# Chunked attention and a token mixer on one core: q, k and v loaded as flat rows, value products in four quadrants, and a new order of work

## The chip, the cores and the metric

The kernel runs on one core of one Trainium2 chip. The metric is the device time of one execution in microseconds (us), as the median of several runs. A profile is one execution taken by the hardware profiler; its span runs from the first to the last instruction. The engines are called PE (matrix products; PEld is its weight load), DVE (vector), ACT (scalar), POOL (GpSimd) and SP (sync). Arithmetic on PE is in f16 with sums in f32 in PSUM, which has eight banks.

## The reference, cut to what matters

Attention inside chunks of 64 tokens, for 8 batches, 8 heads, 576 tokens (nine chunks) and a head size of 64, then a mixer over all tokens of a batch:

```python
scores = scale * np.matmul(q_c, k_c.transpose(0, 1, 2, 4, 3))   # (B, H, 9, 64, 64)
scores = scores - np.max(scores, axis=-1, keepdims=True)
attn = np.exp(scores)
attn = attn / (np.sum(attn, axis=-1, keepdims=True) + 1e-09)
out = np.matmul(attn, v_c)
x = out.transpose(0, 2, 1, 3).reshape(B, S, H * D)              # (8, 576, 512)
wq = x @ w_q                                                    # (8, 576, 64)
wk = x @ w_k
W_tok = scale * np.einsum('bsd,btd->bst', wq, wk)
mixed = np.einsum('bst,btd->bsd', W_tok, x)
return (np.maximum(mixed, 0.0) @ w_out).astype(np.float32)
```

Inputs and output are f32. q, k and v are 9.4 MB each, the output is 9.4 MB, `w_out` is 1 MB.

## The kernel before, in words

**Order.** `ORDER` is a list of words written out by hand, such as `SC2.0@0` or `OE5:A`: a kind of step, a batch (or an output tile), a part, the first PSUM bank after `@`, the engine after `:`. The loop at the end of the kernel goes through it and issues each step's instructions; every engine runs its own in that order. The mixer is computed as `wq @ (wk^T x)`, so nothing of size 576 x 576 is made.

**Loads** (`load`, L100 to L124). q, k and v are brought in by POOL, which casts f32 to f16 on the way. The heads of a batch are split in two halves: heads 0 to 3 go to partitions 0 to 63 (f = 0), heads 4 to 7 to partitions 64 to 127 (f = 1). Each transfer fills one half, 64 partitions. q and k go in blocks of 512 rows, eight consecutive rows to a partition (L113), and the last 256 rows of a half as a tail of four rows to a partition (L120). v goes one row of 64 numbers to a partition (L108). A batch takes ten transfers or more. All q and k have a buffer (four pairs of batches, `qk`); v has five buffers, `vt`, and batch n + 5 is loaded when the value products of batch n have been issued. The output tiles are staged in the `qk` buffers of batches that are done, and the first store waits for the last load (`last["held"]`).

**v buffers** (`clear`, L126). A `vt` buffer holds, for each pair of chunks g, 132 columns: the values of half 0 on partitions 0 to 63 in columns 0 to 63, those of half 1 on partitions 64 to 127 in columns 66 to 129, a column of ones behind each (it gives the sum of the exponentials), and zeros elsewhere. DVE clears two of the five buffers and POOL three, between the loads.

**A batch** runs through these steps.

- TR (`tr`, L156; its instruction is at L174): DVE transposes 32 x 32 blocks of q and k from `qk` to `qkT`, as f32 words that hold two f16. For q the columns are also reordered so that the writes are runs of eight words; for k and the tails the writes go in steps of eight or four words. Three parts with 512, 512 and 128 columns, for q and k each.
- SC (`sc`, L179, product at L188): scores of 64 keys by 64 queries. The head size lies in 32 words of two numbers (e = 0, 1), so a score is the sum of two products with 32 rows. Four strips of 32 rows (i = 0 to 3) are used in turn.
- EX (`ex`, L196): ACT takes the exponential out of PSUM into `est`; for 1024 columns with a reorder that undoes q's.
- PV (`pv`, L205, product at L217): one product for a pair of chunks, one of each half: 128 rows (64 keys of each), 64 queries, 130 columns of `vt`. Forty in a batch.
- RN (`rn`, L227): DVE takes the reciprocals of the sums (L231) and multiplies (L232), giving `xn`, the attention output in f16.
- DT (`dt`, L241): DVE transposes `xn` in 32 x 32 blocks to `xq`.
- PJ (`pj`, L245), EP, DU, WT, EW: the projections with `w_q` and `w_k` (64 products on four strips), their copy out of PSUM, a copy of half of it to the other partitions, and the transposition of `wk` on PE with its copy by DVE.
- GM (`gm`, L284), EG: `wk^T x` and its copy out.
- MX, RL: `wq` times that, and the relu into `rmx`, four parts (ACT, at the end DVE too).
- OM, OE (`oe`, L347): the product with `w_out`, 128 tokens at a time (36 tiles, four products of 512 columns each), the copy out of PSUM, and, when a group of tiles is full, its store by SP (L357).

Scores and value products of a batch, its mixer and output tiles of earlier batches are interleaved, so that PE has work while DVE and ACT work on other parts.

## Time and profile before

| what | value |
|---|---|
| runs | 142.51, 146.77 and 146.08 us; median 146.08 |
| span of the profiled execution | 144.6 us; the times around the span are not listed for it, so this stands for its time, 1.5 us under the median |
| PE | 2312 products with as many weight loads |
| DVE, ACT | 172 and 105 instructions |
| last load lands, first store is issued | at 97 us, at 98.4 us |
| last product ends, last copy out of PSUM starts | 138.5 us |

How to read the rows. A row of the groups gives line, engine, operation, what it writes and reads with partitions x elements, the count, then busy time in us and the mean ns of one, then the idle time of the engine before them and what ended it. A row of the timeline gives start, duration, engine, line, operation, count, and in brackets the idle time before it. A row of the chain of waits gives start, duration, engine, line, count; "issue" is time in which the engine waited for nothing that the profile shows. A row of the windows gives the stretch, its length, busy time and instruction count of each engine, the granted clock of PE, the DMA share and GB/s. GB/s count the bytes written, f16 for the loads.

### The profile page before, as it was taken

To read this page: it belongs to the slowest core of one execution; us is meant where nothing else is said; L and a number is where in the kernel's file an instruction comes from. 1 tells how busy PE (TensorE), PEld (TensorE's weight loads), DVE (VectorE), ACT (ScalarE), POOL (GpSimd) and SP (SyncE) were. 2 spreads that over 40 slices of the span, in tenths; PEclk is the share of its full clock that TensorE was granted. 3 is DMA by queue.
4 is the path that set the end of the run, shared out by engine and by line. 5 is a ranking of instruction groups with operands and counts; after the bars stand their busy time and mean duration, and the time that the engine had idled before them with its cause. 6 is when DMAs were issued, how large, how long until landed. Compare 5 with 4: busy or idle time off the path is not lost.

```text
span 144.6 us, 5246 instructions
## 1 busy us (share of the span) xinstructions
PE 99.5 (69%) x2312; PEld 58.9 (41%) x2312; DVE 90.5 (63%) x172; ACT 65.5 (45%) x105; POOL 68.8 (48%) x105
## 2 busy tenths in 40 slices
PE   0022763147697849987699874998984999989920
PEld 0021642036455523655445552355453356643400
DVE  5643791384896649888917989378971597455100
ACT  4410301032746624584343625467752376564630
POOL 7957996994699781793783883600000000000000
PEclk9999999999999995998557999689999599999997
DMA  4999899999699999999999999995996050441295
GB/s 98 151 186 191 54 172 187 144 184 203 79 148 146 201 154 184 173 144 182 177 151 195 180 147 197 174 102 233 410 408 268 17 208 5 175 190 74 75 360 218
DMA packets 51782, 25.11 MB, mean 174 GB/s; under 512 B 38608, under 2 KB 49872, under 8 KB 51760
## 3 DMA queue, kind: packets, MB, share of 16 engines
q0 software_dynamic: 49056, 14.69, 103.2%
q1 hardware_dynamic: 2704, 10.09, 17.6%
q8 instruction: 18, 0.29, 0.8%
q14 instruction: 4, 0.03, 0.1%
HBM read 29.62 MB, written 9.44 MB: 270 GB/s over the span
## 4 chain that ended last, share of the span: by engine, by line
PE 54%; DMA 12%; issue 10%; POOL 9%; ACT 7%; DVE 3%; DVEq 0%; ACTq 0%; POOLq 0%
PE pb L339 26%; PE pb L217 9%; DMA vt<-in_v_dram 8%; PE pb L188 7%; PE pb L250 5%; DMA qk<-in_q_dram 5%; POOL qk L113 4%; PE pb L288 4%; ACT est L203 3%; POOL vt L108 3%; PE pb L303 2%; ACT rmx L317 2%; POOL vt L129 1%; POOL qk L120 1%; DVE xn L232 1%
## 5 line engine op out<-in xcount | busy, mean ns | idle before, releaser
L339 PE MATMUL pb<-wout,rmx 128*128 128x512 f16 x144 | 40.2, 420 | 0.9 <-ACT rmx L317 0.9
L174 DVE STREAM_TRANSPOSE qkT<-qk 128x512 f32<-128x512 f32 (+1 forms) x48 | 31.2, 717 | 13.7 <-DMA qk<-in_q_dram 11.1
L188 PE MATMUL pb<-qkT 32*64 32x64 f16 x1152 | 16.7, 210 | 24.6 <-DVE qkT L174 18.1
L203 ACT ACTIVATE est<-pb 128x1024 f16<-128x1024 f32 (+1 forms) x24 | 19.2, 813 | 30.6 <-PE pb L188 30.1
L232 DVE TENSOR_TENSOR xn<-pb,rec 128x768 f16<-128x768 f32 (+1 forms) x32 | 26.4, 824 | 4.3 <-PE pb L288 3.2
L351 ACT COPY qk<-pb 128x512 f32<-128x512 f32 x34 | 19.8, 587 | 20.1 <-PE pb L339 19.4
L188 PEld LDWEIGHTS <-qkT 32*64 32x64 f16 x1152 | 13.8, 123 | 28.5 <-DVE qkT L174 19.9
L217 PE MATMUL pb<-vt,est 128*64 128x130 f16 x320 | 18.7, 258 | 9.6 <-ACT g L297 2.8
L108 POOL DMA_DIRECT2D vt<-in_v_dram x20 | 20.9, 1055 | 7.8 <-DMA qk<-in_q_dram 3.2
L339 PEld LDWEIGHTS <-rmx 128*128 128x128 f16 x144 | 13.5, 108 | 16.3 <-issue 4.0
L217 PEld LDWEIGHTS <-est 128*64 128x64 f16 x320 | 12.9, 127 | 16.5 <-issue 7.9
L317 ACT ACTIVATE rmx<-pb 128x576 f16<-128x576 f32 x28 | 17.0, 653 | 4.6 <-PE pb L303 4.5
L231 DVE RECIPROCAL rec<-pb 128x12 f32<-128x12 f32 (+1 forms) x32 | 6.6, 206 | 16.3 <-PE pb L217 16.1
L243 DVE STREAM_TRANSPOSE xq<-xn 128x384 f32<-128x384 f32 (+1 forms) x32 | 15.2, 497 | 0.7
L120 POOL DMA_DIRECT2D qk<-in_k_dram x16 | 8.3, 530 | 11.8 <-DMA vt<-in_v_dram 10.4
L250 PE MATMUL pb<-xq,wpj 32*128 32x160 f16 x512 | 12.3, 242 | 1.9 <-DVE xq L243 1.2
L113 POOL DMA_DIRECT2D qk<-in_q_dram x18 | 11.2, 627 | 2.6 <-DMA qk<-in_k_dram 1.3
L250 PEld LDWEIGHTS <-wpj 32*128 32x128 f16 x512 | 10.1, 97 | 5.3 <-issue 5.0
L261 ACT CAST wqk<-pb 128x640 f16<-128x640 f32 x8 | 5.5, 693 | 14.0 <-PE pb L250 14.0
L113 POOL DMA_DIRECT2D qk<-in_k_dram x18 | 11.1, 633 | 0.0
L120 POOL DMA_DIRECT2D qk<-in_q_dram x16 | 8.8, 575 | 1.1 <-DMA vt<-in_v_dram 1.1
L303 PE MATMUL pb<-wqk,g 64*128 64x288 f16 x32 | 8.4, 309 | 1.2 <-ACT rmx L317 0.7
(24 smaller groups left out, 57.5 us busy)
## 6 DMA issues: line engine op xcount, KB each, us to landing
out_dram<-qk SPq DMA_DIRECT2D x11, 768.0 KB, 4.3
qk<-in_q_dram POOLq DMA_DIRECT2D x14, 256.0 KB, 7.1
qk<-in_k_dram POOLq DMA_DIRECT2D x14, 256.0 KB, 8.5
vt<-in_v_dram POOLq DMA_DIRECT2D x12, 288.0 KB, 7.1
vt<-in_v_dram POOLq DMA_DIRECT2D x8, 144.0 KB, 5.3
out_dram<-qk SPq DMA_DIRECT2D x3, 256.0 KB, 2.0
qk<-in_q_dram POOLq DMA_DIRECT2D x4, 128.0 KB, 5.1
qk<-in_k_dram POOLq DMA_DIRECT2D x4, 128.0 KB, 5.7
```

Of the source, the lines that this page charges most:

```text
L108: d = nc.gpsimd.dma_start(vt[b % NVB][rows, NCH * lo : NCH * hi, f * (D + 2) : f * (D + 2) + D], src.rearrange("(c p) d -> p c d", p=CH)[: ...
L113: d = nc.gpsimd.dma_start(qk[b // 2][rows, b % 2, s, 8 * lo : 8 * hi].rearrange("p (t r) d -> p t (r d)", r=8), src[0 : 4 * 512].rearrange ...
L120: d = nc.gpsimd.dma_start(qk[b // 2][rows, b % 2, s, 32:36].rearrange("p r d -> p (r d)"), src[4 * 512 :].rearrange("(p r) d -> p (r d)", ...
L174: nc.vector.transpose(out=to, in_=frm)
L188: nc.tensor.matmul(ps[half : half + CH, bank + i % 2, at : at + CH], lhsT=qkT[b % 2][rows, 1, tok, e], rhs=qkT[b % 2][rows, 0, tok, e], st ...
L203: nc.scalar.activation(dst, src, AF.Exp, scale=scale_attn)
L217: nc.tensor.matmul(ps[CH * o : CH * o + CH, bank + m // 3, at : at + VP].rearrange("p (f d) -> p f d", f=2)[:, :, 0 : D + 1], lhsT=e, rhs= ...
L232: nc.vector.tensor_tensor(out=xn[b % 2][:, 6 * u : 6 * u + nb * ns // 2].rearrange("p (k n) (f d) -> p k (n f) d", k=nb, f=2), in0=xv[:, : ...
L250: nc.tensor.matmul(ps[:, bank + i, 0 : NJ * 32], lhsT=wpj[32 * i : 32 * i + 32, 4 * f + kk, e, :], rhs=xq[b % 2][32 * i : 32 * i + 32, NJ ...
L317: nc.scalar.activation(dst, src, AF.Relu, scale=scale_moe)
L339: nc.tensor.matmul(ps[:, bank, :], lhsT=c[:, r], rhs=wout[:, i, :], start=(i == 0), stop=(i == NI - 1),)
L351: nc.scalar.copy(os_, ps[:, bank, :])
```

## The change

Ahead of attention, rows are addressed flat over heads, (h s), without the split in halves. A load spans 128 partitions: q and k take four consecutive rows to a partition, for all 4608 rows in nine blocks of 512, without a tail; v takes one row to a partition. Batch 0 comes in six transfers, the others in three, and `w_out` in one. There are eight v buffers of 66 columns per chunk (64 values, a one, a gap), without zeros, so that all loads are issued at the start without waiting for a buffer, and the clears go; only the ones are set, by DVE.

A chunk of 64 rows now lies on half of the partitions: chunk n = 9 h + c is at partitions 64 (n mod 2) on. So a value product takes 64 rows, and its result goes to partitions 64 (c mod 2) on: four quadrants of PE's array, 72 products of 65 columns in a batch. Scores go to four units of 32 or 40 products, each of which uses two strips of rows and both halves of the columns. q and k are transposed by steps of their own (TQ, TK) in parts of 512 and 640 columns, all in the form of the old tails. There are four exponentials of 512 and 640 columns without reorder, four normalisations of equal size, two back transposes of 640 columns. The order is new as a whole; some EW, EG, RL and OE change engine. New words `ZZ` are filler products of 512 columns on a tile of ones whose result nobody reads: 79, of which 67 stand ahead of the first projection.

```diff
 ORDER = """
-TR0.0 SC0.0@0 EX0.0 PV0.0@2 TR0.1 TR0.2 SC0.1@4 RN0.0 SC0.2@6 EX0.1 DT0.0 PV0.1@0 EX0.2 PV0.3@2 RN0.1 PV0.2@4
-RN0.3 DT0.1 DT0.3 RN0.2 DT0.2 PJ0@0 TR1.2 TR1.0 SC1.2@6 EP0 EX1.2 SC1.0@4 TR1.1 WT0@0 EX1.0 PV1.3@1 EW0 RN1.3
...
+ZZ1@0 ZZ1@1 ZZ1@2 ZZ1@3 ZZ1@4 ZZ1@5 ZZ1@6 ZZ1@7 TQ0.0 TK0.0 ZZ13@0 SC0.0@0 SC0.1@2 EX0.0 EX0.1 ZZ4@4 PV0.0@2 RN0.0
+TQ0.1 TK0.1 ZZ14@4 SC0.2@2 SC0.3@0 EX0.2 EX0.3 ZZ1@4 PV0.1@2 RN0.1 ZZ1@4 PV0.2@0 PV0.3@4 DT0.0 RN0.3 TQ1.0 TQ1.1
+RN0.2 DT0.1 TK1.0 ZZ26@6 PJ0@0 TK1.1 SC1.0@4 EP0 SC1.1@6 EX1.1 WT0@0 DU0 SC1.3@2 EW0:D EX1.0 SC1.2@6 GM0@0 EX1.2
...
-    vt = [sb.tile([P, NG, VP], F16, name=f"vt{i}") for i in range(NVB)]
+    vt = [sb.tile([P, NG, VP], F16, name=f"vt{i}") for i in range(B)]
...
-    halves = [x.rearrange("b (f h) s d -> b f (h s) d", f=2) for x in (q, k, v)]
+    flat = [x.rearrange("b h s d -> b (h s) d") for x in (q, k, v)]
...
+            src = flat[s][b]
+            if s == 2:
+                d = nc.gpsimd.dma_start(
+                    vt[b][:, lo:hi, 0:D],
+                    src.rearrange("(g p) d -> p g d", p=P)[:, lo:hi, :],
+                )
+            else:
+                d = nc.gpsimd.dma_start(
+                    qk[b // 2][:, b % 2, s, 4 * lo : 4 * hi].rearrange(
+                        "p (t r) d -> p t (r d)", r=4
+                    ),
+                    src.rearrange("(t p r) d -> p t (r d)", p=P, r=4)[:, lo:hi],
+                )
...
+    def tr(b, x, s):
+        at = (slice(0, 16), slice(16, NG), slice(0, 8), slice(8, 16))[x]
+        nc.vector.transpose(
+            out=qkT[b % NQT][:, s]
+            .bitcast(F32)
+            .rearrange("p n o -> p (n o)")[:, 32 * at.start : 32 * at.stop]
+            .rearrange("p (t w r) -> p t r w", r=4, w=32),
+            in_=qk[b // 2][:, b % 2, s, at].bitcast(F32).rearrange("p (t r) w -> p t r w", r=4),
+        )
...
     def sc(b, u, bank):
+        pi = u % 2
+        for x, t in enumerate(((0, 1, 2, 3), (4, 5, 6, 7, 8))[u // 2]):
+            for e in range(2):
+                for row in (2 * pi, 2 * pi + 1):
+                    for eta in range(2):
+                        rows = slice(32 * row, 32 * row + 32)
+                        half = slice(CH * eta, CH * eta + CH)
+                        tok = slice(P * t + CH * eta, P * t + CH * eta + CH)
                         nc.tensor.matmul(
+                            ps[half, bank + row % 2, CH * x : CH * x + CH],
+                            lhsT=qkT[b % NQT][rows, 1, tok, e],
+                            rhs=qkT[b % NQT][rows, 0, tok, e],
...
     def pv(b, u, bank):
+        for c in range(NCH):
+            for h in (2 * u, 2 * u + 1):
+                n = NCH * h + c
+                eta, o = n % 2, c % 2
+                t, row = n // 8, (n % 8) // 2
+                e = est[b % 2][2 * (t >= 4) + row // 2][
+                    CH * eta : CH * eta + CH, row % 2, t % 4 if t < 8 else 4
+                ]
+                at = VP * (c // 2)
                 nc.tensor.matmul(
+                    ps[CH * o : CH * o + CH, bank + h % 2, at : at + D + 1],
                     lhsT=e,
+                    rhs=vt[b][CH * eta : CH * eta + CH, n // 2, 0 : D + 1],
...
+    def idle(n, bank):
+        for _ in range(n):
+            nc.tensor.matmul(
+                ps[:, bank, :], lhsT=unit[:, 0:P], rhs=unit[:], start=True, stop=True
+            )
+
+    nc.vector.memset(unit[:], 1.0)
+    for i in range(B):
+        nc.vector.memset(vt[i][:, :, D : D + 1], 1.0)
+    load(0, ["q0-4", "k0-4", "v0-18", "q4-9", "k4-9", "v18-36"])
     small_weights()
-    clear(2, "G")
-    load(1, ['q0-4', 'k0-4', 'q4-5', 'k4-5', 'v0-4'])
+    load(1, ["q0-9", "k0-9", "v0-36"])
+    make_identity(nc, ident[:])
     weights()
...
+    for b in range(2, B):
+        load(b, ["q0-9", "k0-9", "v0-36"])
```

More of the change, by code (lines that the diff above doesn't have):

```diff
@@ L40 @@
+OE33:A OE35:A
 """.split()
@@ L62 @@
     NJ = (NCH + 1) // 2
[L63 to L65 removed]
+    NG = H * NCH // 2
     NI = DM // P
     HS = S // 2
[L68 removed]
+    VP = D + 2
     scale_attn = 1.0 / math.sqrt(D)
@@ L141 @@
+            last["i"] = d
+    def weights():
+        nc.gpsimd.dma_start(wout[:], moe_w_out.rearrange("(i p) m -> p i m", p=P))
     wpf = rmx[1][:].rearrange("p i n -> p (i n)").bitcast(F32)[0:32, 0 : 16 * 2 * DH].rearrange(
@@ L391 @@
             banks[kind, n, x] = int(bank)
-        if kind == "TR":
-            tr(n, x)
+        if kind == "TQ":
+            tr(n, x, 0)
+        elif kind == "TK":
+            tr(n, x, 1)
         elif kind == "SC":
@@ L399 @@
             pv(n, x, banks["PV", n, x])
-            left[n] = left.get(n, 4) - 1
-            if left[n] == 0 and n + NVB < B:
-                load(n + NVB, VL[n + NVB])
-                if n + NVB + 1 < B:
-                    load(n + NVB + 1, QKL)
         elif kind == "RN":
@@ L430 @@
             oe(n, banks["OM", n, 0], eng)
+        elif kind == "ZZ":
+            idle(n, int(bank))
     tc.add_manual_dep(
```

247 lines of the change are left out of this document (77 added, 170 removed).

## The prediction, on record before the changed kernel was seen

> **What bounds the kernel now.** I read the page's engine shares and chain first, then one window per stage, then the single waits.
>
> ```profile
> span 144.6 us, 5246 instructions
> PE 99.5 (69%) x2312; PEld 58.9 (41%) x2312; DVE 90.5 (63%) x172; ACT 65.5 (45%) x105; POOL 68.8 (48%) x105
> q8 instruction: 18, 0.29, 0.8%
> PE 54%; DMA 12%; issue 10%; POOL 9%; ACT 7%; DVE 3%; DVEq 0%; ACTq 0%; POOLq 0%
> ```
>
> ```profile
> 28.00:62.00 34.00, 25.56 (x660) 15.81 (x661) 25.31 (x49) 16.48 (x28) 24.58 (x39) 0.95 1.58 162
> 62.00:97.00 35.00, 28.19 (x697) 16.31 (x699) 26.89 (x52) 17.48 (x29) 21.18 (x32) 0.80 1.74 168
> 97.00:139.00 42.00, 37.76 (x721) 20.46 (x720) 23.78 (x46) 25.17 (x43) 0.00 (x0) 0.96 0.48 190
> ```
>
> The columns of the windows are PE, PEld, DVE, ACT and POOL busy, granted clock, DMA share and GB/s. No engine is full over the whole run. Up to 62 us the transposes wait for q and k, which the next rows show; after that the loads are ahead, and PE, 81% to 90% busy, sets the pace.
>
> ```profile
> 7.02 0.71 DVE L174 STREAM_TRANSPOSE qkT<-qk 128x512 f32<-128x512 f32 x1
> 7.89 1.09 DVE L174 STREAM_TRANSPOSE qkT<-qk 128x512 f32<-128x512 f32 x1 [0.16 <-DMA qk<-in_k_dram]
> 28.08 1.90 DVE L174 STREAM_TRANSPOSE qkT<-qk 128x128 f32<-128x128 f32 x3 [0.30 <-DMA qk<-in_k_dram]
> 62.07 1.12 DVE L174 STREAM_TRANSPOSE qkT<-qk 128x512 f32<-128x512 f32 x1 [0.85 <-DMA qk<-in_k_dram]
> ```
>
> The four rows are q and k of batch 0, k of batch 1 and k of batch 4: DVE stood still until they landed. The last one is the last time that a load holds the kernel up.
>
> The "issue" tenth of the chain is a second bound. Two rows of PE's timeline (first and last of the six relu-layer products) and the chain around them:
>
> ```profile
> 48.40 0.29 PE L303 MATMUL pb<-wqk,g 64*128 64x288 f16 x1
> ...
> 48.79 0.28 PE L303 MATMUL pb<-wq,g 64*128 64x288 f16 x1
> ```
>
> ```profile
> 43.08 0.98 PE pb L339 x4
> ...
> 45.12 1.05 issue
> 46.17 0.28 PE pb L188 x10
> 46.45 0.47 PE pb L217 x12
> 46.92 0.66 PE pb L288 x10
> 47.59 0.24 PE pb L217 x4
> 47.83 0.68 PE pb L188 x64
> ...
> 49.60 0.99 PE pb L217 x21
> 50.60 2.14 issue
> 52.74 0.28 PE pb L217 x3
> ```
>
> Both waits split a group of products in the middle (6 and 10 of 16, 21 and 3 of 24), with nothing that releases them. Between them lie 10 + 12 + 10 + 4 + 64 + 6 + 21 = 127 products, that is 254 instructions with a weight load each. The page's instruction queue made 18 transfers of 0.29 MB together, and PE runs 2312 + 2312 = 4624 instructions, 257 to a transfer. So I read these waits as PE standing at the end of a block of 256 instructions whose successor has not arrived. The longest of each kind:
>
> ```profile
> PE pb L188 <- issue: 6.4, 4, 2.5
> PE pb L217 <- ACT g L297: 2.8, 2, 1.4
> PE pb L217 <- issue: 2.1, 1, 2.1
> ```
>
> The middle row is put down to ACT, but both waits lie a multiple of 256 instructions from the others. Seven waits, 11.3 us: 0.63 us for each of 18.1 blocks, about 1.6 us where a block ends in a run of short products.
>
> ```profile
> 68.00:77.50 9.50, 8.37 (x190) 0.50 1.69 171
> ...
> sum 18.30, PE 17.17; mean PE 4.29
> ```
>
> Last, in four stretches, 18.3 us in all, the granted clock was 0.50; PE was busy for 17.17 us of them.
>
> **The change part by part.** The sum is made against the span of 144.6 us, which is 1.5 us under the median of the three runs (146.08); I add the 1.5 back at the end.
>
> *Loads.* Ninety transfers become 28, and q and k rows go in runs of four (512 B in f16) where they went in runs of eight (1024 B) with tails. Three stretches of the DMA queues and two idle ones (the windows' last column):
>
> ```profile
> DMA packets 632, 0.61 MB, mean 205 GB/s; under 512 B 32, under 2 KB 632, under 8 KB 632
> ```
>
> ```profile
> DMA packets 298, 0.20 MB, mean 200 GB/s; under 512 B 45, under 2 KB 297, under 8 KB 297
> ```
>
> ```profile
> DMA packets 2268, 0.29 MB, mean 144 GB/s; under 512 B 2268, under 2 KB 2268, under 8 KB 2268
> ```
>
> ```profile
> 16.50:18.50 2.00, 1.55 (x28) 1.30 (x24) 1.05 (x3) 0.96 (x2) 2.00 (x5) 1.00 0.38 26
> ...
> 37.50:39.50 2.00, 1.10 (x20) 0.64 (x14) 1.93 (x4) 1.92 (x4) 1.98 (x2) 1.00 0.20 26
> ```
>
> ```profile
> L129 POOL MEMSET vt<- 128x2376 f32 x3 | 6.3, 2096 | 0.0
> ```
>
> Over 16 engines a 1024 B packet costs 16 x 1024 / 205 = 80 ns and a 128 B packet of v 16 x 128 / 144 = 14 ns. A straight line gives 42.5 ns for 512 B, 193 GB/s. It is 205 at best; solving the mixed row in the middle for its short packets, with its waste, gives about 161 at worst. A batch is 1.18 MB of q and k and 0.59 MB of v: 6.1 + 4.1 = 10.2 us, all of it back to back, since POOL's clears (2.1 us each, during which nothing is issued and the queues run dry to 26 GB/s) and the waits for v buffers are gone. POOL's own work per batch falls under 10 us, so it hides under the transfers. Batch 4's k needs 5 x 6.1 + 4 x 4.1 + 2.6 for wout = 49.5 us plus start and landing; batch 0's first 0.52 MB (2.6 us) had landed at 7.9, so at most 5.3, and I take 4.5 because no clear and fewer issues stand ahead. It lands at 54 where it landed at 62.1: **-8.1 us** (-9 at 205 GB/s; -2 at 161). Batch 1's k lands at 2 x 6.1 + 4.1 + 4.5 = 20.8 instead of 28.1.
>
> *What is late next.* DVE works 90.5 / 8 = 11.3 us a batch, about 11.0 without its clears, longer than the loads' 10.2. Over batches 2 to 4 it falls behind by 3 x 0.8: **+2.4 us** (0 if its idle time covers it; 5 if PE's waits add to it).
>
> *Transposes and their layout.* The rows of DVE and ACT that price them:
>
> ```profile
> L174 DVE STREAM_TRANSPOSE qkT<-qk 128x128 f32<-128x128 f32 x16 | 5.4, 393 | 8.4 <-DMA qk<-in_q_dram 7.2 <-DMA qk<-in_k_dram 1.2
> L243 DVE STREAM_TRANSPOSE xq<-xn 128x384 f32<-128x384 f32 x24 | 13.0, 563 | 0.5
> L243 DVE STREAM_TRANSPOSE xq<-xn 128x128 f32<-128x128 f32 x8 | 2.4, 302 | 0.2
> L203 ACT ACTIVATE est<-pb 128x1024 f16<-128x1024 f32 x16 | 16.3, 1026 | 20.7 <-PE pb L188 20.1 <-ACT qk L351 0.4
> L203 ACT ACTIVATE est<-pb 128x256 f16<-128x256 f32 x8 | 3.1, 388 | 10.0 <-PE pb L188 10.0
> ```
>
> q lost nothing in the old layout (0.71 us for 512, against k's 1.09), but both now take the form of the tails, whose 128 columns cost 393 ns where a plain transpose costs 302. On k's line, (1090 - 393) / 384 = 1.8 ns an element, 640 columns take 1.32 us: a batch is 2 x (1.09 + 1.32) = 4.82 instead of 2 x (0.71 + 1.09 + 0.39) = 4.38, +0.44. The back transposes, two of 640 (302 + 512 x 1.02 = 824 ns) for three of 384 and one of 128, give back 0.34. Four batches lie behind the last load wait: **+0.4 us** (0 to +1.8). Four exponentials of 512 and 640 columns cost 2 x 0.60 + 2 x 0.71 = 2.62 for 2.44, and the normalisation the same columns; ACT is 53% busy from 28 us on and hides it (0.7 us if not). The engines of EW, EG, RL and OE change hands one for one: zero, covered by DVE's and ACT's idle time, 3 us if that is gone.
>
> *Value products.* Forty of 128 rows and 130 columns become 72 of 64 rows and 65 columns in four quadrants. Now twelve take 0.47 us, 39 ns each, 1.57 a batch. The nearest row for the new ones is that of the scores, 64 columns each, 64 products in 0.68 us, 10.6 ns; the upper end is the old 39 ns. I take 13 ns, since a quadrant must load and stream by itself (52 ns over four): 0.94 a batch, **-2.5 us** over the four batches behind the load waits (-3.2; +5 at 39 ns). That two column halves of the same rows run together is shown: a product of 512 columns takes 0.98 / 4 = 245 ns, so 130 columns alone would need 62 ns, and they took 39.
>
> The Trainium skill, "TensorE: Matmul & The Clock Gate", Part 3, says that a weight load overlaps products in flight only when its row group differs, which speaks against this order of quadrants and of scores; the 39 ns do not bear that out for column halves, and the rule's own result is a rival below.
>
> *Instructions.* PE's go from 4624 to 2 x 2647 = 5294 (256 more value products, 79 filler products): 2.6 blocks more, at 0.63 us each **+1.6 us** (0 if the extra blocks end in long products, +6 at the 2.1 us above).
>
> The Trainium skill, "Runtime: NRT & Kernel Launch", Instruction fetch mechanics, calls the crossing of such a block mostly hidden; by that the term would be 0 and the time 138.3. The 2.14 us wait says otherwise here.
>
> *Fillers.* 67 of 79 filler products stand ahead of the first projection. At 245 ns the 26 before it take 6.4 us; they hide under the wait for batch 1's k (20.8) and cost up to 4 us if the clock is at half there. DVE's transposes of q1 now stand ahead of the last normalisation of batch 0, so projection 0 waits for that landing too; the scores of batch 1 had to wait for it anyway. The eight ones columns and the filler operand delay DVE by no more than the two old clears. SP's stores wait for the last load and so start near 89 instead of 98, at no cost on the path. The new order as such I put at 0 (-4 to +4).
>
> Sum: -8.1 + 2.4 + 0.4 - 2.5 + 1.6 = -6.2; 144.6 becomes 138.4, and with the 1.5, **139.9 us**.
>
> **The rivals.**
>
> *Blocks set the pace (slower).* Counting the new order in blocks of 256 from the same start, eleven boundaries after batch 0 fall behind runs of scores and value products; now seven waited. If each waits 2.3 us (2.14 and 2.5 are above), that is 25.3 us instead of 11.3 + 1.6: 152 us. It turns slower than 149 from a mean of 2.0 us. For it: the value products finish faster, so less time for the fetch. Against: loads end sooner, and today's mean is 1.6.
>
> *Row groups serialise.* A score strip does 16 products in 0.64 us, 40 ns each; the new units use two strips at a time, so scores would cost 2.9 a batch instead of 1.5, and value products 36 x 40 = 1.44 instead of 0.94: +7.6 over four batches, less 1.6 since the fetch then has time: 146. Against it stand the 39 ns. This is the page's rule named above.
>
> *Loads come no earlier.* At 161 GB/s a batch takes 11.4 us, batch 4's k lands at 60, and DVE keeps pace: 139.9 + 6.1 - 2.4 = 143.6. For it: packets half as long.
>
> *The waits shrink.* Fillers hold the clock (half of the 8.6 us that 17.17 at half clock cost, 4) and the waits at blocks fall from 11.3 to about 6 as packets ahead of the fetch get shorter: 131. Against: the fetch waited 2.5 us in the stores' time too.
>
> **How the numbers follow.** Forecast 0.36 (134 to 144), blocks 0.17, row groups 0.12, loads 0.13, shrinking waits 0.22. The range of 130 to 150 leaves out the upper half of the block rival and the tail below. Two per cent, about what a measurement of this kernel can tell from no change, is 143.2 to 149.0. Faster: nearly all of the forecast, the shrinking waits and half of the loads rival, 0.62; same: row groups, the other half, the edges, 0.21; slower: 0.17.
>
> **What would show it.** Right: batch 1's k at about 21 us, batch 4's near 54, the last load near 89; q and k at 185 to 200 GB/s; 18 value products in about 0.24 us; a 512-column transpose at 1.09 us; "issue" waits near 13 us. Wrong: a k4 landing after 58; score units of 32 products at over 0.5 us; "issue" over 20 us; projection 0 later than 26 us.

## The result, and the profile after

The changed kernel took 151.55 us (median of 4 runs, 150.47 to 152.51), beside 146.43 us (142.51 to 147.84) for the kernel before on the same chip: a ratio of 1.059 with a 95% interval of 1.041 to 1.077. Executions of one kernel fall into a faster and a slower group some per cent apart, so the ratios here and below are taken over the faster ones alone and the medians over all, and the trace of the kernel before, with its span of 144.6 us, is by that length one of the slower. It is slower by some 6%, where 139.9 us had been forecast, and it lies above the forecast's range of 130 to 150. The profiled execution took 152.51 us, 150.7 of them in the span.

Page of the changed kernel: span, engines, granted clock in 40 slices, the instruction queue, the chain by engine.

```profile
span 150.7 us, 5753 instructions
...
PE 119.1 (79%) x2647; PEld 65.5 (43%) x2647; DVE 93.0 (62%) x146; ACT 65.6 (44%) x110; POOL 33.7 (22%) x34
...
PEclk9999879965599857996555697589955999999999
...
q8 instruction: 20, 0.33, 0.8%
...
PE 59%; issue 13%; DVE 9%; ACT 8%; DMA 7%; POOL 2%; DVEq 0%; ACTq 0%; POOLq 0%
```

The same clock line of the kernel before:

```profile
PEclk9999999999999995998557999689999599999997
```

"issue", time in which the engine waited for nothing that the profile shows, is 13% of the chain (10% before). The clock is at half in more slices, 51.2 us against 20.5, but these two figures can't be set side by side. The trace of the kernel before has no clock record ahead of 36.9 us, and the page counts that stretch as full speed. The products there came at the rate of half clock; these are 64 score products ahead of 36.9 us and 64 behind it:

```profile
33.64 1.07 PE L188 MATMUL pb<-qkT 32*64 32x64 f16 x64
...
43.99 0.71 PE L188 MATMUL pb<-qkT 32*64 32x64 f16 x64
```

Score products came every 13.2 ns from the first one at 9.04 us on, and every 8.2 ns later. From 36.9 us on the comparison is fair: 42.0 us at half clock against 20.5. The longest "issue" pieces and their neighbours in the chain:

```profile
19.70 6.33 PE pb L333 x26
26.03 1.28 PE pb L214 x64
...
29.03 3.70 issue
...
48.31 3.57 issue
...
63.24 1.01 PE pb L214 x45
64.26 4.23 issue
68.49 0.71 PE pb L214 x18
...
79.51 1.65 issue
```

26 filler products, then projection 0 at 26.03 us (19.3 us before). The wait of 4.23 us cuts projection 3 in two, 45 products and 18. Counted in the trace's records of PE (each product, its weight load, and a few semaphore records), these waits end at instructions 961, 1729, 2241 and 2753 of 5294, all 193 more than a multiple of 256, as do three shorter ones: 15.7 us in seven waits, 11.3 us in seven before. I call what lies between two such places a block.

DVE's waits for loads, after and before:

```profile
DVE qkT L139 <- DMA qk<-in_q_dram: 4.9, 2, 3.3
```

```profile
DVE qkT L174 <- DMA qk<-in_q_dram: 11.1, 3, 5.2
DVE qkT L174 <- DMA qk<-in_k_dram: 2.5, 5, 0.9
```

So the loads did come earlier: by the trace's completion signals, k of batch 1 landed at 23.1 us (28.0 before) and k of batch 4 at 56.0 (62.0 before); the last packet of a load ended at 88.6 (98.0 before). 8.7 of the 13.6 us in the last two rows are gone. Both waits of the first row are for batch 0's q; from batch 1 on no transpose waits for a load.

The work behind did not follow. The first transpose of batch 4's k, which waited for its load until 62.07 us before, is this piece of the chain in the changed kernel, 16.8 us after its k had landed:

```profile
72.78 1.08 DVE qkT L139
```

The new order has put somewhat more work ahead of it. But at 62.07 us itself PE was no further either: it had begun 512 score products, three projections and 34 output products in the kernel before, and 500, two and 36 in the changed one.

Where did the time go? Two windows each, cut about where the loads end (columns as above: busy time of PE, PEld, DVE, ACT, POOL, granted clock, DMA share, GB/s). After:

```profile
26.00:88.00 62.00, 46.35 (x1228) 26.72 (x1227) 39.26 (x56) 27.09 (x47) 16.95 (x13) 0.72 1.79 180
88.00:146.00 58.00, 50.54 (x1149) 29.10 (x1137) 39.68 (x65) 32.29 (x56) 0.00 (x0) 0.88 0.37 146
```

Before:

```profile
19.00:97.00 78.00, 56.57 (x1419) 34.05 (x1422) 55.67 (x110) 34.66 (x57) 53.35 (x78) 0.89 1.68 167
97.00:138.00 41.00, 37.31 (x720) 20.46 (x720) 23.78 (x46) 24.45 (x42) 0.00 (x0) 0.96 0.48 188
```

The 0.89 in the first row of the kernel before counts 19 to 36.9 us as full clock, which it was not. When its loads end, the kernel before has 720 products left, the changed one 1149. Counted at the block that begins there:

| | before | after |
| --- | --- | --- |
| block begins, us | 97.23 | 87.85 |
| instructions behind it | 1359 of 4624 | 2285 of 5294 |
| projections, score and output products left | 3, 232, 84 | 4, 432, 96 |
| from there to the last product, us | 41.2 | 58.4 |
| PE busy / idle in it, us | 37.5 / 3.7 | 51.0 / 7.5 |
| of it at half clock, us | 3.4 | 13.7 |

The block begins 9.4 us earlier, and what is left takes 17.2 us longer: the last product ends 7.8 us later (146.3 instead of 138.5), of which a shorter tail (4.4 us for 6.2) gives 1.7 back: the 6.1 us between the spans. The end of the loads came nearer; the work did not come with it.

Are these waits the fetching of instructions? The trace has the packets of the instruction queue, one of 16384 bytes for each block. Each of the seven waits of either kernel ended 1.3 to 1.6 us after such a packet had ended, and the packet itself took 0.9 to 1.4 us, with loads or without. So they are waits for the next block of instructions. What differs is when its packet starts:

| kernel, block begins at, us | next block's packet starts after, us | it takes, us | from its end to the next block, us |
| --- | --- | --- | --- |
| after, 45.41 | 4.09 | 0.97 | 1.41 |
| after, 62.02 | 4.10 | 1.07 | 1.30 |
| after, 74.69 | 4.03 | 0.97 | 1.48 |
| after, 87.82 (first behind the loads) | 0.92 | 0.93 | 1.41 |
| after, 105.24 | 1.29 | 0.96 | 1.32 |
| before, 103.22 (stores running) | 4.81 | 0.94 | 1.44 |

### The profile page after: what moved, and what is told of

Its sections match the earlier page's. It is cut to its first block, busy times and chain, and to the rows that moved or that the text cites. A ratio compares the mean times of both kernels' runs of the same rounds, so it can differ in the third digit from the quotient of the medians.

```text
span 150.7 us, 5753 instructions
## 1 busy us (share of the span) xinstructions
PE 119.1 (79%) x2647; PEld 65.5 (43%) x2647; DVE 93.0 (62%) x146; ACT 65.6 (44%) x110; POOL 33.7 (22%) x34
## 4 chain that ended last, share of the span: by engine, by line
PE 59%; issue 13%; DVE 9%; ACT 8%; DMA 7%; POOL 2%; DVEq 0%; ACTq 0%; POOLq 0%
PE pb L306 27%; PE pb L214 8%; DMA qk<-in_q_dram 7%; PE pb L333 6%; PE pb L156 6%; PE pb L183 4%; PE pb L252 3%; ACT rmx L286 3%; DVE xn L195 3%; DVE qkT L139 3%; PE pb L270 3%; ACT est L166 2%; ACT wqk L223 1%; POOL qk L111 1%; DVE rec L194 1%
## 5 line engine op out<-in xcount | busy, mean ns | idle before, releaser
L166 ACT ACTIVATE est<-pb 128x512 f16<-128x512 f32 (+1 forms) x32 | 19.5, 652 | 23.7 <-PE pb L156 19.2
L195 DVE TENSOR_TENSOR xn<-pb,rec 128x640 f16<-128x640 f32 x32 | 26.4, 824 | 1.2
L333 PE MATMUL pb<-unit 128*128 128x512 f16 x79 | 24.9, 462 | 1.5 <-DVE unit L337 1.5
L194 DVE RECIPROCAL rec<-pb 128x10 f32<-128x10 f32 x32 | 6.6, 206 | 27.5 <-PE pb L183 25.4
L183 PE MATMUL pb<-vt,est 64*64 64x65 f16 x576 | 13.0, 220 | 7.2 <-issue 4.7
L183 PEld LDWEIGHTS <-est 64*64 64x64 f16 x576 | 10.2, 127 | 11.5 <-issue 7.0
L204 DVE STREAM_TRANSPOSE xq<-xn 128x640 f32<-128x640 f32 x16 | 13.4, 836 | 0.4
L333 PEld LDWEIGHTS <-unit 128*128 128x128 f16 x79 | 8.2, 111 | 12.3 <-issue 5.4
L270 PE MATMUL pb<-wq,g 64*128 64x288 f16 x32 | 9.8, 363 | 0.0
L111 POOL DMA_DIRECT2D qk<-in_k_dram x9 | 8.8, 973 | 1.5 <-DMA qk<-in_q_dram 1.5
## 6 DMA issues: line engine op xcount, KB each, us to landing
wout<-in_moe_w_out_dram POOLq DMA_DIRECT2D x1, 512.0 KB, 18.1
```

Of the source, the lines that this page charges most:

```text
L166: nc.scalar.activation(est[b % 2][u].rearrange("p i n c -> p i (n c)"), ps[:, bank : bank + 2, 0:n], AF.Exp, scale=scale_attn,)
L183: nc.tensor.matmul(ps[CH * o : CH * o + CH, bank + h % 2, at : at + D + 1], lhsT=e, rhs=vt[b][CH * eta : CH * eta + CH, n // 2, 0 : D + 1] ...
L195: nc.vector.tensor_tensor(out=xn[b % 2][:, 2 * u : 2 * u + 2], in0=xv[:, :, :, 0:D], in1=rc[:, :, :, None].broadcast_to([P, 2, NJ, D]), op ...
L270: nc.tensor.matmul(ps[:, bank + h, 0:HS], lhsT=g16[b % 2][CH * h : CH * h + CH, i * P : i * P + P], rhs=src[CH * h : CH * h + CH, half * H ...
L333: nc.tensor.matmul(ps[:, bank, :], lhsT=unit[:, 0:P], rhs=unit[:], start=True, stop=True)
```

## The experiments

I began with two theories: A, that PE stands at the ends of blocks because the next block's transfer is held up behind the loads; B, that the new order's dependences cost it by themselves. C (the clock follows the use of the array), F (under the loads the blocks set a pace, whatever is in them) and others came later. Ratios are against the kernel before on the same chip; the changed kernel itself was not run again beside its variants, so they are set beside it by their ratios. Where only a few lines of a repeated edit are shown, the rest is as the expectation says.

**Loads taken away.** Both kernels without the loads of batches 2 to 7, computing on the data of batches 0 and 1. The clears of the v buffers that are no longer used go too, and the stores start at 40 to 42 us instead of 89 to 98.

```diff
-        src = qk[b // 2][:, b % 2].bitcast(F32)
+        src = qk[0][:, b % 2].bitcast(F32)
...
-    for b in range(3, NVB):
-        load(b, QKL + VL[b])
-    load(NVB, QKL)
```

> The kernel before, without the loads of batches 2 to 7 (their steps compute on the q, k and v of batches 0 and 1, so the output is not the reference's). Theory A (PE stands at the end of blocks of 256 instructions because the next block's transfer is held up behind the loads, and the clock halves after such waits): the seven long waits of 11.3 us fall under 3 us, the time at half clock from 20 us to under 10, and the kernel takes about 128 us. Theory B (the waits are dependences between the engines, and loads matter only where a transpose waits for them): the gain is the 13.6 us that DVE waited for q and k, less what compute makes up, about 140 us, and the long waits of PE stay near 11 us.

> The changed kernel, without the loads of batches 2 to 7 in the same way. Theory A: the seven waits of 15.7 us fall under 3 us, the time at half clock from 51 us to under 20, and the kernel takes about 126 us, level with the quiet kernel before or under it. Theory B (the new order and layout are worse by themselves): it stays about 5 us above the quiet kernel before, at 140 us or more, with the clock at half for some 50 us.

Measured: 127.57 us for the one (145.08 for the kernel before, ratio 0.886, interval 0.875 to 0.898), 142.45 and 145.07 us for the other. In the kernel before the seven waits are gone, and the clock is at half for 3.4 us from its first clock record at 35.6 us on: A holds there. In the changed kernel the first block behind instruction 3009 begins at 74.97 us instead of 87.85, but 7.8 us of waits at blocks' ends stay, and 33 us at half clock from 35.6 us on. The first transpose of batch 4's k is at 62.72 us, later than in the kernel before with all its loads.

```profile
PE pb L157 <- issue: 3.0, 2, 1.9
PE pb L184 <- issue: 1.9, 2, 1.1
...
PE pb L215 <- issue: 1.6, 1, 1.6
```

So A alone does not tell the two kernels apart: the changed kernel has a floor of its own some 15 us above the old one's, and above the forecast of 139.9 us. What the order, the layout and the clock each have in that floor was not measured. It has blocks of little but scores and value products that end in a wait, loads or not, though without loads they begin only 2.8 to 5.3 us apart.

**The order mended by hand, and without fillers.** Eleven output tiles moved between score units (first block); all but the first eight filler products taken out (second).

```diff
-SC2.0@0 TK2.1 EX2.0 WT1@4 DU1 SC2.3@6
+SC2.0@0 OM0@6 TK2.1 EX2.0 WT1@4 DU1 OE0:A OM1@5 SC2.3@6
```

```diff
-TQ0.0 TK0.0 ZZ13@0 SC0.0@0
+TQ0.0 TK0.0 SC0.0@0
```

> The changed kernel with the same instructions; ten output tiles are moved later, from where they stood in a row to between the units of scores. Theory A: blocks of nearly only scores, which PE ran through in under 3 us, get long products, so the waits fall from 15.7 to about 10 us and the time to about 147 us. Theory B: the tiles no longer fill PE's time while DVE transposes, so the time stays at 151.5 us or grows by 2.

> The changed kernel without the filler products except the first eight: 142 of PE's instructions fewer. Theory A: half a block less and shifted boundaries, waits within 2 us of 15.7 us, time 149 to 152 us. If the fillers hold the clock: the time at half clock grows from 51 us, and the kernel gets slower by 3 us or more.

Measured: 154.84 us (1.071, 1.058 to 1.085) and 155.43 us (1.077, 1.066 to 1.088). Mixed, the waits at blocks' ends fell to 12.9 us and waits on DVE took their place. Without the fillers the clock stood at half for 82 us instead of 51. Whether fillers pay is not shown: the interval touches the changed kernel's (1.041 to 1.077).

**The clock.** In stretches of 3.41 us, the step in which the recorded clock changes, I set the use of the array (rows times columns in use times columns moved, as a share of the full array at full speed) beside the clock of the next stretch. Theory C came from six kernels, and I tried to move it by the value products' rows alone.

```diff
-                    rhs=vt[b][CH * eta : CH * eta + CH, n // 2, 0 : D + 1],
+                    rhs=vt[b][:, n // 2, 0 : D + 1],
```

```diff
-                    lhsT=e,
+                    lhsT=e[0:CH],
```

> The changed kernel with its value products over all 128 rows instead of 64: each product multiplies two neighbouring 64-token chunks at once, and the ninth chunk of a head also fills the unused half of its output columns, so the attention values are sums over the wrong chunks. The number of instructions, the columns that each product moves, the order and the loads stay as they were; only the part of the TensorE array that is in use doubles in these products.
>
> Theory C (the clock follows the use of the array): cut into stretches of 3.41 us, the records of the six kernels so far show a stretch at half clock mostly after one in which rows times columns in use times columns moved came to less than about a third of what the full array does in that time at full speed. Of the changed kernel's stretches, those from 89.2 us (0.30, with 36 value products), 106.2 us (0.28, with 54) and 68.7 us (0.34, still half after it, with 60) come over a third when value products count twice. Some 30 of its 51 us at half clock should go, leaving 20 to 25 us, and with about a third of that the time: 140 to 143 us.
>
> Theory B (the order's own waits, whatever the array does): the clock falls after the waits as before, 45 to 50 us at half, and the time stays at 151 us.

> The kernel before with its value products over 64 of the 128 rows: half of each sum is left out (the zeros of the block-diagonal v are replaced by 0.0625, so that all numbers stay finite). The count, the columns moved, the order and the loads stay; the part of the array that is in use halves in these products.
>
> Theory C: the stretches that stay just over a third now, from 36.9 us (0.33), 43.7 us (0.35) and 81.3 us (0.33) of its trace, fall under it, so that the time at half clock goes from 20.5 us to 35 to 45 us and the kernel gets 4 to 8 us slower: 150 to 154 us.
>
> Theory B: the waits set the clock and the waits stay: 20 to 24 us at half, 145 to 147 us.

Measured: 155.24 us (1.070, 1.060 to 1.081) and 145.27 us (0.986, 0.975 to 0.996). Neither told what it was made for. With all rows in use, neighbours that share a half of the columns no longer ran beside each other: 36 took 1.16 us where the changed kernel's take 0.51 (rows below, both at full clock), and 10.9 us of added busy time hid the rest. In the other, the time at half clock hardly moved. As a forecast of these two times C failed.

```profile
88.80 1.16 PE L187 MATMUL pb<-vt,est 128*64 128x65 f16 x36
```

```profile
87.60 0.51 PE L183 MATMUL pb<-vt,est 64*64 64x65 f16 x36
```

As an observation it stands: over all 607 stretches of the seventeen kernels, the clock was at half after every one of the 127 with a use under 0.25, and full after 353 of the 354 at or over 0.4; one limit of 0.32 tells 587 of them rightly, the best of seven limits on PE's busy share 506.

**Parts of the sum, on the kernel before.** The clears of three v buffers moved from POOL to DVE, meant to have the loads issued earlier (the loads of batches 2 to 5 become a word of the order, ahead of the first projection); and 40 more score products a batch.

```diff
-    clear(2, "G")
...
+        if kind == "CL":
+            clear(n, "D")
+        elif kind == "LD":
+            for later in range(2, NVB):
+                load(later, QKL + VL[later])
+            load(NVB, QKL)
```

```diff
+        if u == 2:
+            for x in range(2, 7):
+                for e in range(2):
+                    for i in range(4):
...
+                            lhsT=qkT[b % 2][rows, 1, 1024 : 1024 + CH, e],
```

> The kernel before with one part of the change alone: the three clears of v buffers 2, 3 and 4 go from POOL to DVE (the first after batch 0's first transposes, the others after its last output transpose), so that POOL issues the loads of batches 2 to 5 without standing at a clear. Nothing else is changed.
>
> The prediction's largest term says that loads which come earlier are worth 8.1 us where the kernel waits for batch 4's k at 62.07 us. By it, k of batch 4 lands at 54 to 57 us and the time comes to 139 to 142 us, with about 2 us of that given back for the 6 us of clears on DVE.
>
> Theory A (the instruction blocks stand in line behind the loads) with theory C: the loads come 4 to 8 us earlier, but PE's waits at the ends of blocks, 11.3 us in the kernel before, stay, and the stretches at half clock with them, so that only the wait for k goes: 143 to 146 us.

> The kernel before with 40 more score products in each batch (they repeat the last tokens' products into unused columns of the same bank, which nothing reads): 320 products, so 640 more PE instructions, 2.5 blocks of 256. At 9.4 ns each the products themselves take 3.0 us in all if none hides.
>
> The prediction's price of 0.63 us a block gives 1.6 us for the blocks: 147 to 150 us with the products.
>
> Theory A: each further block that is crossed under the loads is a wait of 1.5 to 2 us and in some cases a stretch at half clock of 3.4 us behind it: 151 to 154 us, with 14 to 16 us of waits at the ends of blocks instead of 11.3.

Measured: 147.11 us (1.008, 0.994 to 1.021) with the clears moved. The edit does not do what was meant by it. POOL issues loads in the order of the words, and the loads of batch 5's v and batch 6's q and k, which stand behind batch 0's value products, now come ahead of those of batches 2 to 4. More bytes had been moved at any time (the queue's 8th megabyte at 53.9 us instead of 56.9), but k of batch 4 landed at 70.0 us instead of 62.0, and DVE waited for it there:

```profile
70.11 1.12 DVE L174 STREAM_TRANSPOSE qkT<-qk 128x512 f32<-128x512 f32 x1 [0.94 <-DMA qk<-in_k_dram]
```

So no run shows by itself what earlier loads are worth to the kernel before. What this one shows is that the landing 8 us later cost at most some 2%, with 6 us of clears on DVE in that too, while the waits at blocks' ends fell from 11.3 to 6.2 us: the time does not follow this landing one for one.

The added products: 150.57 us (1.040, 1.032 to 1.049), 5.4 us. They are busy for 3.9 us of PE's time, waits at blocks' ends rose to 15.2 us while DVE's wait for q fell from 11.1 to 7.6: the two waits stand in for each other.

**Layout, order and start apart.** The changed layout and loads in the old order, without and with 40 fillers at the start; the changed order with batch 1's transposes moved back; the value products in another order of quadrants.

```diff
-ZZ1@7 TQ0.0 TK0.0 ZZ13@0 SC0.0@0 SC0.1@2 EX0.0 EX0.1 ZZ4@4 PV0.0@2 RN0.0 TQ0.1 TK0.1 ZZ14@4
+ZZ1@7 TQ0.0 TK0.0 SC0.0@0 SC0.1@2 EX0.0 EX0.1 PV0.0@4 TQ0.1 TK0.1 SC0.2@6 SC0.3@0 RN0.0
```

```diff
-RN0.2 DT0.1 TK1.0 ZZ26@6 PJ0@0 TK1.1
+RN0.2 DT0.1 TQ1.0 TK1.0 TQ1.1 ZZ13@6 PJ0@0 TK1.1
```

```diff
-        for c in range(NCH):
-            for h in (2 * u, 2 * u + 1):
+        for c0 in range(0, NCH, 2):
+            for h, c in [(h, c) for h in (2 * u, 2 * u + 1) for c in (c0, c0 + 1) if c < NCH]:
```

> The changed kernel's loads, tiles and products, put into the order of the kernel before: each step of the old order is replaced by the changed kernel's steps on the same data (a score unit of eight chunks by two of four, the small third unit by what is in the new second pair, the output transposes by two a batch), PSUM banks are handed out anew, and of the filler products only the first eight stay. Nothing is left out of the result.
>
> Theory O (the new order costs what the earlier loads bring): with the old order PE gets its large output products between the small ones again; projection 0 comes at 20 to 22 us instead of 25.96, the loads stay at their last landing near 88 us, and the time is 138 to 143 us, under that of the kernel before.
>
> Theory L (the layout costs it: 512 more PE instructions are two more blocks to fetch, and quarter-array products let the clock fall): the waits at the ends of blocks stay at 12 us or more and the half clock at 40 us or more: 147 to 152 us.

> The kernel with the changed layout and the old order once more, now with 40 filler products ahead of projection 0, at the places where the changed kernel has them. Without them its clock stood at half from 8.4 to 39.1 us.
>
> Theory W: with the clock at full speed in that stretch it gains 2 to 4 us: 147 to 149 us.
>
> Theory F: the blocks set the pace there, and the fillers are 80 more instructions: 150 to 153 us.

> The changed kernel with one thing moved at its start: the two transposes of batch 1's q go behind batch 0's last output transpose on DVE, with 13 filler products instead of 26 ahead of projection 0.
>
> Theory P (the start is where the time went: projection 0 came at 25.96 us instead of 19.3 us, and from there to the last product both kernels took about 120 us): projection 0 at 23 to 24 us and a time that follows it, 148.5 to 149.5 us.
>
> Rival: the products after it wait for batch 1's transposes or for the next block in any case, so that the time stays at 151 to 152 us.

> The changed kernel with the value products of a unit issued in another order, so that each differs from the one before it in its half of the rows and its half of the columns: the quadrants come as (0,0), (1,1), (1,0), (0,1) instead of (0,0), (1,0), (1,1), (0,1). The same products are made.
>
> The prediction's term of 13 ns a product took four products to overlap; the changed kernel's took 18 to 20 ns. If it is the order of the quadrants that keeps two neighbours apart, they take 13 to 15 ns, 72 of them 0.4 us less a batch, and the time is 149 to 151 us. If a product of 65 columns is bound by its own issue, they stay at 18 to 20 ns and the time at 151 to 152 us.

Measured: 151.14 us for the old order (147.62 to 152.87, too wide for a ratio), 150.41 with its fillers (1.049, 1.038 to 1.060), 153.70 with the start moved (1.063, 1.055 to 1.072), 152.15 with the other quadrants (1.052, 1.044 to 1.059). Theory O, that the order alone costs it, falls as the whole cause; how the changed layout does in the old order without loads was not run. Theory P, that the start costs it, falls too: projection 0 came 4.2 us earlier (21.8 us), and 0.7 us was left of that at the end of the third long wait, which ends at 64.26 + 4.23 = 68.5 us in the changed kernel. With the start moved it ends at 67.8 (the second row):

```profile
48.67 3.02 issue
63.49 4.29 issue
```

and in the old order with fillers at 67.5:

```profile
64.22 3.23 issue
```

The quadrants' order changed nothing, 36 products in 0.51 us as before. The fillers in the old order took the time at half clock from 72 us to 44, and the two medians lie 0.7 us apart, less than the spread of either: time at half clock is not lost one for one.

**Instructions against work.** Half of the score products left out of each kernel; output products of half the columns.

```diff
-            for e in range(2):
+            for e in range(1):
```

```diff
-                rhs=wout[:, i, :],
+                rhs=wout[:, i, 0 : DM // 2],
```

> The changed kernel with half of its score products: of the two that add up to a score (the even and the odd numbers of a head's 64), only the even ones are made, so the scores are sums over 32 numbers. That takes 1152 of 5294 PE instructions, 4.5 blocks of 256, but only some 6.5 us of PE's busy time. Loads, order, transposes and everything else stay.
>
> Theory F (while the loads run, PE gets one block of 256 instructions every 6.1 to 6.6 us, whatever is in it; in the changed kernel eleven fetches start between 14.97 and 85.35 us, and at the end of the loads 57 per cent of the instructions have run, where the kernel before had 71 per cent at the end of its own): 4.5 blocks fewer leave 1130 instructions instead of 2285 at the end of the loads, and the time falls by two to three times the work that is left out: 132 to 139 us.
>
> Theory W (PE's work and its clock set the time): it falls by at most the work left out: 145 to 147 us.

> The same half of the score products left out of the kernel before: 1152 of 4624 PE instructions, about 7 us of PE's busy time.
>
> Theory F: blocks come no faster, but 13.6 of them do what 18 did; the waits at their ends and the waits for k are on the same stretch, and the later one is left, so that the time falls by more than the work: 133 to 138 us.
>
> Theory W: 139 to 142 us.

> The changed kernel with output products of 256 columns instead of 512: the right half of each output tile is left out (what the bank holds is copied). No instruction goes; PE's busy time falls by up to 20 us, of which 13 us lie behind the last load (16 of the 24 groups of output products start after 88 us) and 7 us ahead of it.
>
> Theory F: what is saved while the loads run is given back at the next block's end, what is saved behind them counts: 137 to 141 us, and the starts of the blocks up to the end of the loads move by less than 2 us.
>
> Theory W: all of it counts, less what the lower use of the array costs in clock: 132 to 136 us.

Measured: 143.13 us (1.000, 0.992 to 1.008), 135.40 us (0.943, 0.933 to 0.953), 147.18 us (1.025, 1.014 to 1.036). The groups that were cut, in the first and the third:

```profile
L156 PE MATMUL pb<-qkT 32*64 32x64 f16 x576 | 8.8, 203 | 8.7 <-issue 5.2
```

```profile
PEclk9999758995559555697576585559955697799996
...
L306 PE MATMUL pb<-wout,rmx 128*128 128x256 f16 x144 | 26.1, 359 | 0.5 <-ACT rmx L286 0.2
```

1152 instructions less, worth 5.6 us of busy time in the changed kernel and 6.7 in the one before, brought 8.4 and 8.8 us at the medians; 14.5 us of busy time less without an instruction brought 4.4. For the kernel before the time is theory F's, 133 to 138, but blocks no longer set its pace: waits at their ends are down to 3.4 us, and PE waits 18.1 us for DVE's transposes. For the changed one F had promised 132 to 139, and the gain fell short of that: with fewer blocks it is held up otherwise, as without loads. In the narrow kernel the loads' part went as F says (the block at instruction 3009 began 1.2 us earlier for 5.6 us less of output products), and both theories were too hopeful behind the loads, where 9.0 us of work less brought 6.0 us: the array was used less, and the time at half clock rose from 51 to 68 us. Of the two runs that lower the use of the array and leave the instructions alone, this one went C's way and the one with the kernel before's value products over 64 rows did not.

The start of the block at instruction 3009, counted in the traces, for the kernels with the changed loads and all their products:

| kernel | us |
| --- | --- |
| changed kernel | 87.85 |
| start moved (projection 0 at 21.8 us) | 87.62 |
| output products half as wide | 86.62 |
| old order, without and with fillers | 87.26, 86.31 |
| other quadrants; tiles mixed | 89.16, 88.69 |
| value products twice as long | 89.53 |
| fillers left out | 89.10 |
| changed kernel without loads | 74.97 |

The last row is for comparison. With the loads the twelfth full block begins at 86.3 to 89.5 us in all of these, though work was added, taken out or moved. Four blocks in a row of the changed kernel began 6.46, 6.20, 6.47 and 6.68 us apart (62.03 to 87.85). It is not so whatever a block holds: with half of the score products, when the same number of instructions is much more work, instruction 3009 comes at 100.1 us in the changed kernel and at 108.2 in the one before, and two blocks of the changed kernel ahead of 62 us took 10.1 us each by their own work. The pace is a least time for a block, and it binds where blocks are short.

## Why the prediction was wrong, step by step

*"Loads": the landings nearly right, the gain wrong. This is the step that failed.* Batch 1's k was forecast for 20.8 us and landed at 23.1, batch 4's for 54 and at 56.0 (6.0 us earlier than before, not 8.1), the last load for 89 and at 88.6. But the 8.1 us were booked in full as a gain, on the reading that the wait for batch 4's k is the last thing that holds the kernel and that all work behind it moves up with the landing. It did not: batch 4's k lay ready from 56.0 us and was first transposed at 72.78, 10.7 us later than in the kernel before. With no loads of batches 2 to 7 at all the changed kernel still took 142.45 and 145.07 us, so no gain in loads could have brought it to 139.9. Two limits lay beneath. While the loads run, blocks that ended in a wait took 5.5 to 6.5 us each in the changed kernel; loads that end 9 us sooner only mean that fewer blocks are done when they end. And without loads there is the changed kernel's own floor, some 15 us above the old one's.

*"What is late next": it was the blocks, not DVE.* The prediction put 2.4 us of DVE there. From batch 1 on DVE waited for no load, and the long waits of PE were for its own instructions, as the packets of their queue show.

*"Instructions": the term that was mis-sized.* Waits at blocks' ends rose by 4.4 us, not by the 1.6 that 0.63 us a block gave. When the loads end, 2285 instructions are left instead of 1359: one block fewer is done, of 670 instructions more. The added products on the kernel before cost 5.4 us for 640 instructions, 1.5 us more than their own 3.9; cutting 1152 brought 2.1 us (before) and 2.8 us (changed) more than their own time.

*"Value products": the rate right, the old price wrong.* From start to start at full clock the new ones come every 12 ns (13 forecast). The old ones come every 30, not 39: the 0.47 us for twelve held the last one's way through the array. The gain at full clock is 40 x 30 - 72 x 12 = 336 ns a batch, not 630.

*"Transposes and their layout": right.* 1.09, 1.32 and 0.824 us were forecast:

```profile
L139 DVE STREAM_TRANSPOSE qkT<-qk 128x640 f32<-128x640 f32 x16 | 20.6, 1316 | 1.7 <-DMA qk<-in_q_dram 1.7
L139 DVE STREAM_TRANSPOSE qkT<-qk 128x512 f32<-128x512 f32 x16 | 17.3, 1090 | 3.5 <-DMA qk<-in_q_dram 3.3 <-DMA qk<-in_k_dram 0.3
L204 DVE STREAM_TRANSPOSE xq<-xn 128x640 f32<-128x640 f32 x16 | 13.4, 836 | 0.4
```

*"Fillers", the clock and the new order at zero.* The sum had no term for the clock. Its reading of four stretches at half clock, 18.3 us, left out the first 28 us of work in the kernel before, which have no clock record and ran at the half rate. From 36.9 us on the changed kernel had 21.5 us more at half clock, and no run shows how much of that is hidden under the waits. The 26 fillers stand on the chain for 6.33 us, but with half of them gone and the transposes moved, 0.7 us of 4.2 was left at 68 us. Behind the loads the changed kernel has thin blocks and stretches of little array use, 13.7 us at half clock there instead of 3.4. That order and layout together were worth 0 is refuted by the floor without loads; which of them made it stays open.

*The rivals.* "Blocks set the pace" gave 152 us, at a chance of 0.17, and names one of the two limits. That its number lies beside the measured 151.55 is luck: it took eleven waits of 2.3 us, and there were seven, 15.7 us together, 4.4 more than before instead of 14. "Row groups serialise" did not occur: scores came every 8.8 ns at full clock.

The rule of the Trainium skill, "Runtime: NRT & Kernel Launch", Instruction fetch mechanics, that crossing such a block is mostly hidden, would have made the time shorter still; this trace disagrees under loads (waits up to 4.23 us), and in part so does the one without them (up to 1.95).

Open is why a block's packet starts so late beside the loads. The traces show that it is its start that is late, by some 3 us, and not the packet that is slow. It does not end with the loads alone: the longest such wait of the kernel before, 2.51 us, ended at 110.4 us, when only stores ran. Nor is it shown that the use of the array sets the clock; the records go with it, two runs were made to move it and did not, and one that was made for something else did. No version here beats the kernel before with its whole work done.

## What to carry to other kernels

A wait that is removed is worth only the distance to the next limit on the same stretch: before booking it, ask what the engine behind it could do at most in that time, its instruction stream included. While heavy loads run, count PE's instructions as well as its microseconds, and give each block of 256 at least as much work as a block takes to arrive (some 6 us here). Ask also what the changed kernel would take with no loads at all: that floor was above the forecast here, and one run shows it. Splitting products into more and smaller ones has two prices to set against its gain: it adds blocks, and it lowers the use of the array with which the clock was seen to go.

## What the runs showed of the hardware

- Under loads that keep the queues full, blocks of 256 PE instructions that ended in a wait mostly took 5.2 to 6.8 us, in some cases 3.2 to 4.7 where the next block's packet had started early. The packet of 16384 bytes itself took 0.9 to 1.6 us; under the loads it started mostly 3.0 to 4.4 us after the block before it had begun, behind them after 0.9 to 1.3 us, or 3.0 to 4.8 where stores ran. Without loads, blocks that began 2.8 to 5.3 us apart still ended in waits of 0.85 to 1.95 us in the changed kernel.
- A trace can lack clock records at its start, and the page then shows full clock: up to 36.9 us score products of the kernel before came every 13.2 ns, behind it every 8.2.
- The clock changed in steps of 3.41 us and was at half in the step after one in which less than about a third of the array's capacity was used (587 of 607 steps). At half, output products came every 427 ns instead of 216, value products 17 instead of 12.
- Products of 65 columns over all rows came every 27 ns when neighbours shared a half of the columns, 64-row products in changing quadrants every 12 ns, and 130-column products over all rows in changing halves every 30 ns.
